# Seven quarter products for the first two blocks of the leading expert, with their gates and the sums around them moved

## The chip, the cores and the metric

The kernel runs on one core of a Trainium2 chip. The metric is device time in microseconds (us) of one execution; a lower time is better. All data are fp32.

## The reference

The first half is a gated linear recurrence over 4 x 8 sequences of 768 steps with a head size of 48. The second half treats the 3072 rows of the result (384 numbers each) as tokens, gives each to the one of 8 experts whose embedding is nearest in angle, and puts it through that expert's two-layer network.

```python
for t in range(S):                       # B, H, S, D = 4, 8, 768, 48
    state = alpha[:, :, t, :, None] * state + einsum('bhd,bhe->bhde', k[:, :, t], v[:, :, t])
    y[:, :, t] = einsum('bhd,bhde->bhe', q[:, :, t], state)
x = y.transpose(0, 2, 1, 3).reshape(B * S, H * D)          # 3072 x 384
logits = (x / (norm(x) + 1e-6)) @ (emb / (norm(emb) + 1e-6)).T / tau
e = argmax(logits, axis=1)
gate = softmax(logits)[arange(N), e]
out = gate[:, None] * (relu(x @ w1[e]) @ w2[e])            # w1: 384 x 1024, w2: 1024 x 384
```

## The kernel before, in words

**Attention part.** The sequence is cut into 24 chunks of 128 steps (`NS`). A software pipeline runs over `s` from 0 to `NS + 2`: in step `s` chunk `s` is turned and its decays are scanned, chunk `s-1` gets its scores and updates the state, chunk `s-2` is mixed (`mix_states`, `mix_chunk`), and chunk `s-3` is turned back into rows (`rows`). At the end of the pipeline, from `s = NS` on, two chunks are in flight at once. Groups of chunks then get their expert (`choose`), their place in the expert's list (`place`), and are sent with an indirect DMA issued by POOL to a sorted copy in memory, `xs` (`to_rows`; the "scatters of rows").

**The leading expert's early blocks.** After chunk 15 it is known that some expert has at least 256 tokens. That expert goes first. Its first two blocks of 128 tokens (`EARLY = 2`) are fetched to `exg` (`fetch_early`) while the attention part still runs, and their first layer (`turn_early`, `first_layer_early`, result `ehT`: 8 slabs of 128 x 256) is spread between the last chunks' work on PE. After the last chunk the counts of the experts are worked out on DVE (`counts`, which ends in `used_i` and `pads`), and blank rows are scattered behind each expert's list (`to_rows(pads...)`).

**Experts.** The second layer of the early blocks runs first: `second_layer` takes 8 products of 384 columns a block. Between the two blocks PE turns the leading expert's last block and half block. Their gates (`gates`: maximum of the logits, squares and root on ACT, exponential on ACT, sum and reciprocal on DVE) are made when the attention part is over. Then `run(i)` goes over the 8 experts: expert 0 has one block left (and a half block in an `If`), the others have three blocks and an `If` for a half block. For three blocks both layers use sums in place of some products. In the second layer, for a pair of blocks, the two blocks are a 2 x 2 grid of quarters of the hidden rows, and `w2` is a 2 x 2 grid of quarters (512 x 192); `second_layer_pair` makes seven products of quarters (Winograd's form) from four sums of hidden quarters (`hT_m`, made by `mix_hidden`) and four sums of weight quarters (`w2_m`, made by `mix_weights`). A product of quarters is four matmuls of 192 columns. Each matmul of fp32 is two instructions in the trace.

**What sets the order.** A planner orders each engine's queue from the program order and its own estimates of readiness. The program pins parts of it: `with tc.issue_after(x)` puts what the block issues behind `x` in `x`'s engine queue, and the lists `pe`, `dve`, `act`, `done_pair` (with `turn_of`, `by_dve`, `by_act`, `pe_turn`) chain calls on one engine. An `If` is one unit in that order.

**Who does which sums before.** `w2_m` for expert 1 is summed by DVE (line 1311); for the experts after it by POOL (line 1313). The sums of the first layer's weights, `w1_m` (`mix_first_weights`), are made by DVE for expert 1 (line 1446), by POOL for the others (line 1357). POOL clears the two tiles `xq` (line 855), into which rows of the experts from 2 on are loaded for turning by DVE.

Of the kernel before, what the change touches and what calls it, by code (L numbers as in the profile page):

```python
# [29 lines left out]
def kernel(  # L30
# [80 lines left out]
    ehT = consts.tile([P, FT, EARLY * P], FP32)  # L111
    NXG = 3
# [113 lines left out]
    with ExitStack() as c1:  # L226
# [79 lines left out]
        def prepare_logits():  # L306

            nc.vector.reciprocal(rtau, rtau)
            e2 = work.tile([E, DM], FP32, name="e2", bufs=1)
            en = work.tile([E, 1], FP32, name="en", bufs=1)  # L310
            nc.scalar.activation(e2, emb, AF.Square, accum_out=en)
# [35 lines left out]
        def choose(g):  # L347

            s0, s1 = GROUPS[g]
            n = s1 - s0  # L350
            shp = [P, n, E]
            l = x_g[g][:, :, LG : LG + E]
            nc.vector.tensor_reduce(
                l.unsqueeze(3), lg_g[g].rearrange("t n j c e -> t n e (j c)"),
                axis=AX.X, op=ALU.add,
            )
            top = work.tile([P, GMAX], FP32, name="top")[:, 0:n]
            nc.vector.tensor_reduce(top.unsqueeze(2), l, axis=AX.X, op=ALU.max)
            win = work.tile([P, GMAX, E], FP32, name="win")[:, 0:n]
            nc.vector.tensor_tensor(win, l, bc(top, shp, 2), ALU.is_equal)  # L360
            nc.vector.tensor_tensor(win, win, bc(first, shp, 1), ALU.mult)
            best = work.tile([P, GMAX], FP32, name="best")[:, 0:n]
            nc.vector.tensor_reduce(best.unsqueeze(2), win, axis=AX.X, op=ALU.max)
            ch = chosen[:, s0:s1]
            nc.vector.tensor_tensor(ch, win, bc(best, shp, 2), ALU.is_equal)
            for s in range(s0, s1):
                eng = nc.vector if {S0 - 1, NS - 1, NS - 2} & set(range(s0, s1)) else nc.gpsimd
                eng.tensor_tensor(before[:, s + 1], before[:, s], chosen[:, s], ALU.add)
# [52 lines left out]
        def counts(n):  # L421
# [20 lines left out]
            nc.vector.scalar_tensor_tensor(  # L442
# [12 lines left out]
            return nc.vector.tensor_copy(used_i, used[0:1])  # L455
# [180 lines left out]
        def mix_chunk(s):  # L636
# [4 lines left out]
            for hh in range(2):  # L641
# [7 lines left out]
                nc.scalar.copy(yT[hh].rearrange("p q t -> p (q t)"), pyx[hh][:, 0:YX])  # L649
# [46 lines left out]
        def first_layer_early(f0, f1):  # L696
            for f in range(f0, f1):
# [6 lines left out]
                nc.scalar.activation(ehT[:, f], ph, AF.Relu)  # L704


# [35 lines left out]
        for s in range(NS + 3):  # L742
# [33 lines left out]
            if NS <= s < NS + 2:  # L776
                with in_turn():
                    first_layer_early(2 * (s - NS), 2 * (s - NS) + 1)
# [16 lines left out]
            if NS <= s < NS + 2:  # L795
                with in_turn():
                    rows(s - 2)
# [31 lines left out]
            if s == NS:  # L829
                with tc.issue_after(st[NS - 1]["masked"].ins):  # L830
                    nc.gpsimd.memset(w1_s[1][:, 0, 0:1], 0.0)
                weights(1)
            for r in rows_of(s):
                g = group_of[r]
                if r == GROUPS[g][1] - 1:
                    with tc.issue_after(st[min(s, NS) - 1]["dve"].ins):
                        choose(g)
                    with behind(s) if s < NS else ExitStack():
                        nc.gpsimd.tensor_copy(x_g[g][:, :, TK], toks[:, slice(*GROUPS[g])])
            if s > NS:  # L840
                with in_turn():
                    first_layer_early(2 * (s - NS) + 2, 2 * (s - NS) + 4)
        with tc.issue_after(st[NS - 1]["dve"].ins):
            routed = [counts(n)]


    with ExitStack() as c3:
        qp = c3.enter_context(tc.tile_pool(name="qp", bufs=1, reuse_waits="tile"))
        xq_s.extend(qp.tile([P, NROW // SQ, DA], FP32, name=f"xq{i}") for i in range(NXQ))
# [10 lines left out]
        yp = c3.enter_context(tc.tile_pool(name="yp", bufs=3, reuse_waits="tile"))  # L860
# [8 lines left out]
        w2_m = wp.tile([P, 4, FT // 2, DM // 2], FP32, name="w2_m")  # L869
        hT_m = xp.tile([P, 4, FT // 2, P], FP32, name="hT_m")  # L870

# [6 lines left out]


# [344 lines left out]
        def second_layer_pair(w2_t, hT, gate, col):  # L1224
# [6 lines left out]
            a, b, d = (bank(j)[:, 0:m] for j in (0, 1, 3))  # L1231
# [28 lines left out]
            gated(y1[:, m:DM], a, g1, u[:, 2])  # L1260
            product(d, s4, b22, False, True)
# [3 lines left out]
            done_pair[:] = pe[0], by_act(nc.scalar.mul, y1[:, 0:m], a, g1)  # L1265
# [34 lines left out]
        def run(i):  # L1300
# [132 lines left out]
        egt = xp.tile([P, EARLY], FP32, name="egt")  # L1433
        esx = xp.tile([P, EARLY], I32, name="esx")
# [49 lines left out]
```

## Time and profile before

| | us |
|---|---|
| median of 3 runs | 392.47 |
| lowest, highest run | 391.89, 395.01 |
| the profiled execution | 391.01 |
| its span, first to last instruction | 389.3 |
| mean granted TensorE clock | 0.998 |

The profiled execution took 391.01 us, of which 1.7 us lie around its span. All times of rows are us from the span's start. PE is the matmul engine; PEld are its weight loads, which overlap the matmuls; DVE, ACT and POOL are the vector, scalar and GpSimd engines; SP issues most DMAs.

### The profile page before, as it was taken

What the parts mean: (1) busy time and instruction counts of PE and PEld (TensorE: products, weight loads), DVE (VectorE), ACT (ScalarE), POOL (GpSimd) and SP (SyncE); (2) the same over time, 40 slices, a digit from 0 to 9 for tenths busy, and PEclk for the clock granted to TensorE, in tenths of its full rate; (3) what the DMA queues carried; (4) which work ended last, traced back from release to release, by engine and by line L of the source; (5) the groups of instructions that cost most, each with busy time, mean ns of one, the idle gap of its engine ahead of it and who ended that gap; (6) DMA issues with size and microseconds to landing.
All of it is one profiled execution on the core that took longest, in us unless ns stands there. A gap on an engine that the chain in (4) does not pass through costs nothing. (4 is left out here: it accounts for less than half of the span.)

```text
span 389.3 us, 12413 instructions
## 1 busy us (share of the span) xinstructions
PE 379.9 (98%) x4596; PEld 338.3 (87%) x4596; DVE 283.9 (73%) x687; ACT 194.3 (50%) x492; POOL 261.7 (67%) x342
## 2 busy tenths in 40 slices
PE   6999999999999999999999999999999999999994
PEld 5889899999999877779989889789979979979974
DVE  7898989889999637992973984963874596795630
ACT  3555565554556544573653734823651492472620
POOL 5365577788776548744829959929957997977201
PEclk9999999999999999999999999999999999999999
DMA  9999999999999996794947768245604810100101
GB/s 138 162 166 166 156 182 197 190 182 198 187 218 174 285 370 231 214 355 97 356 109 285 212 197 287 46 154 182 180 19 175 296 28 18 43 2 17 40 19 46
DMA packets 131181, 64.05 MB, mean 165 GB/s; under 512 B 113319, under 2 KB 127920, under 8 KB 130344
## 3 DMA queue, kind: packets, MB, share of 16 engines
q1 hardware_dynamic: 127008, 52.92, 58.2%
q0 software_dynamic: 3728, 10.16, 7.3%
q8 instruction: 43, 0.70, 0.8%
q14 instruction: 26, 0.21, 0.2%
q10 hardware_dynamic: 376, 0.05, 0.1%
HBM read 53.85 MB, written 11.45 MB: 168 GB/s over the span
## 5 line engine op out<-in xcount | busy, mean ns | idle before, releaser
L1035 DVE TENSOR_TENSOR hT<-hT,pq 128x384 f32<-128x384 f32 x84 | 44.0, 549 | 35.9 <-PE pq L1143 28.4
L889 POOL DMA_INDIRECT out_dram<-y,sx x25 | 29.7, 1188 | 54.3 <-ACTq L1381 20.3
L538 POOL TENSOR_TENSOR qs<-qc,a 128x512 f32<-128x512 f32 x24 | 30.8, 1283 | 30.0 <-DVE a L534 20.8
L1143 PE MATMUL pq<-xT_m,w_m 128*128 128x192 f32 x252 | 44.4, 326 | 0.0
L1017 PE MATMUL pyo<-w,hT 128*128 128x384 f32 x128 | 42.6, 486 | 0.0
L1143 PEld LDWEIGHTS pq<-xT_m,w_m 128*128 128x128 f32 x252 | 41.4, 190 | 0.2
L1017 PEld LDWEIGHTS pyo<-w,hT 128*128 128x128 f32 x128 | 24.1, 190 | 14.8
L1040 ACT ACTIVATE hT<-hT 128x384 f32<-128x384 f32 x56 | 26.3, 515 | 15.2 <-DVE hT L1035 14.6
L1097 POOL TENSOR_TENSOR w_m<-w,w_m 128x256 f32<-128x256 f32 x42 | 31.1, 753 | 2.0 <-PE pq L1143 0.6
L1055 POOL TENSOR_TENSOR w_m<-w 128x768 f32<-128x768 f32 x12 | 23.9, 1991 | 11.7 <-PE pq L1240 11.7
L335 POOL DMA_INDIRECT xs<-x,dest x24 | 24.3, 1013 | 10.4 <-DVE dest L392 5.0
L534 DVE TENSOR_TENSOR_SCAN a<-pa,ini 128x512 f32<-128x512 f32 x24 | 29.3, 1222 | 1.0
L505 DVE TENSOR_TENSOR_SCAN r<-pa,inr 128x511 f32<-128x511 f32 x24 | 29.3, 1220 | 0.7
L1097 POOL TENSOR_TENSOR w_m<-w 128x256 f32<-128x256 f32 x36 | 28.2, 800 | 2.2 <-DVE xT_m L1113 1.4
L1240 PE MATMUL pq<-w_m,hT_m 128*128 128x192 f32 x168 | 28.6, 327 | 0.0
L1240 PEld LDWEIGHTS pq<-w_m,hT_m 128*128 128x128 f32 x168 | 27.4, 190 | 0.5 <-issue 0.5
L217 PE MATMUL pyx<-sm,vt 128*64 128x128 f32 x384 | 26.3, 279 | 0.0
L217 PE MATMUL sc<-qs,kr 64*64 64x128 f32 x768 | 25.6, 271 | 0.0
L217 PEld LDWEIGHTS pyx<-sm,vt 128*64 128x64 f32 x384 | 20.5, 136 | 4.1 <-issue 3.6
L1040 ACT ACTIVATE hT<-pq 128x384 f32<-128x384 f32 x28 | 13.7, 490 | 17.8 <-PE pq L1143 17.8
L1247 DVE SCALAR_TENSOR_TENSOR y<-pq,gt,u 128x192 f32<-128x192 f32 x21 | 8.6, 416 | 18.8 <-PE pq L1240 12.8
L1240 PEld LDWEIGHTS pq<-w,hT 128*128 128x128 f32 x112 | 18.4, 190 | 4.5 <-issue 2.6
(231 smaller groups left out, 986.2 us busy)
## 6 DMA issues: line engine op xcount, KB each, us to landing
w<-in_moe_w_dram SPq DMA_DIRECT2D x12, 1536.0 KB
w<-in_moe_w_dram SPq DMA_DIRECT2D x16, 384.0 KB
at<-in_alpha_dram SPq DMA_DIRECT2D x24, 192.0 KB
kt<-in_k_dram SPq DMA_DIRECT2D x24, 192.0 KB
qt<-in_q_dram SPq DMA_DIRECT2D x24, 192.0 KB
vt<-in_v_dram SPq DMA_DIRECT2D x24, 192.0 KB
xg<-xs SPq DMA_DIRECT2D x22, 196.5 KB
xq<-xs SPq DMA_DIRECT2D x72, 48.0 KB
```

What stands on the lines that cost most here:

```text
L217: last["pe"] = nc.tensor.matmul(*args, **kwargs)
L335: ins = nc.gpsimd.indirect_dma_start(out=xs, out_offset=bass.IndirectOffsetOnAxis(ap=rows, axis=0), in_=x, in_offset=None, bounds_check=E ...
L505: nc.vector.tensor_tensor_scan(r[:, L - 2 :: -1], pa[:, L - 1 : 0 : -1], inr[:, L - 2 :: -1], 1.0, ALU.mult, ALU.add,)
L534: d["a_scan"] = by_dve = nc.vector.tensor_tensor_scan(a, pa, ini, 0.0, ALU.mult, ALU.add)
L538: by_pool = nc.gpsimd.tensor_tensor(qs.rearrange("p n t -> p (n t)"), d["qc"], a, ALU.mult)
L889: ins = nc.gpsimd.indirect_dma_start(out=out, out_offset=bass.IndirectOffsetOnAxis(ap=col, axis=0), in_=y, in_offset=None, bounds_check=N - 1,
L1017: pe[:] = [nc.tensor.matmul(py, lhsT=hT[:, f], rhs=w2_t[:, f], start=(f == 0), stop=(f == FT - 1),)]
L1035: dve[:] = [call(*args, **kwargs)]
L1040: act[:] = [call(*args, **kwargs)]
L1097: by(w[to], w[x], w[y], op)
L1143: pe[:] = [nc.tensor.matmul(to[:, f], lhsT=w[left][:, f * P : (f + 1) * P], rhs=x[right], start=start and f == 0, stop=stop, skip_group_ch ...
L1240: pe[:] = [nc.tensor.matmul(to, lhsT=left[:, f], rhs=right[:, f], start=start and f == 0, stop=stop and f == n - 1, skip_group_check=True,)]
```

## The change

- The early blocks' second layer is made by `second_layer_pair`: seven products of quarters, four sums of `w2_s[0]`'s quarters and four sums of `ehT`'s quarters, all eight on DVE. Two weight sums (`t1`, `t3`) are pinned into the attention part's last steps; the other six stand in a chain on DVE behind `counts`, and the sums of expert 1's first layer stand behind that chain.
- The turning of the leading expert's other rows and their gates (`prepare_lead`) are called in the middle of the pair, behind its fifth product on PE.
- The early blocks' own gates (`early_gates`) are made in step `s = NS`: squares on ACT behind the first early slab and behind the mixing of a late chunk, exponential on ACT behind that chunk's rows, the rest on DVE.
- The sums of expert 1's `w2` go from DVE to POOL, behind the early blocks' scatters and that of expert 0's last block (`done_pair`).
- `xq` is cleared by four copies on ACT in place of two memsets on POOL.
- In memory: `w2_m`, `xq` and `hT_m` are the first tiles after the attention part's tiles are given up; the small tile `e2` is replaced by part of a tile `vt`; the four banks `pq` are laid out first, and the pair uses banks 3, 1 and 2.

```diff
@@ in the attention part @@
+        def early_gates():
+            ...
+            v.tensor_reduce(top_e.unsqueeze(2), l, axis=AX.X, op=ALU.max)
+            v.tensor_scalar(none_e, token, 1.0, float(FAR), ALU.is_lt, ALU.mult)
+            v.scalar_tensor_tensor(
+                out=esx.unsqueeze(2), in0=token, scalar=-1.0, in1=none_e,
+                op0=ALU.add, op1=ALU.add,
+            )
+            v.tensor_tensor(sh_e, l, bc(top_e, shp, 2), ALU.subtract)
+            for t in range(EARLY):
+                nc.scalar.activation(
+                    x2_e, exg[:, t, 0:DM].rearrange("p (h d) -> p h d", d=D), AF.Square,
+                    accum_out=sq_e[:, t],
+                )
+                yield
+            nc.scalar.activation(sq_e, sq_e, AF.Sqrt)
+            v.tensor_scalar(sq_e, sq_e, 1e-6, None, ALU.add)
+            v.reciprocal(sq_e, sq_e)
+            yield v.tensor_tensor(sh_e, sh_e, sq_e.to_broadcast(shp), ALU.mult)
+            nc.scalar.activation(sh_e, sh_e, AF.Exp)
+            yield
+            v.tensor_reduce(egt.unsqueeze(2), sh_e, axis=AX.X, op=ALU.add)
+            v.tensor_scalar(egt, egt, 1e-9, None, ALU.add)
+            yield v.reciprocal(egt, egt)
...
+            if s == NS:
+                gating = early_gates()
+                with tc.issue_after(turned_up.ins), tc.issue_after(st[NS - 1]["dve"].ins):
+                    next(gating)
...
-                    mix_chunk(s - 2)
+                    cols_done = mix_chunk(s - 2)
+                if s == NS:
+                    with tc.issue_after(cols_done.ins):
+                        next(gating)
+                        scaled = next(gating)
...
-                    rows(s - 2)
+                    copied = rows(s - 2)
+                if s == NS:
+                    with tc.issue_after(copied.ins):
+                        next(gating)
...
-                        choose(g)
+                        group_done = choose(g)
+                    if s == NS:
+                        with tc.issue_after(group_done.ins):
+                            early_gated = next(gating)
@@ between the parts @@
-        for x in xq_s:
-            with tc.issue_after(routed[-1].ins):
-                nc.gpsimd.memset(x, 0.0)
...
+        for j in range(4):
+            ps_q.tile([P, 512], FP32, name=f"pq{j}")
@@ second_layer_pair(w2_t, hT, gate, col, middle=None) @@
-            a, b, d = (bank(j)[:, 0:m] for j in (0, 1, 3))
+            a, b, d = (bank(j)[:, 0:m] for j in ((3, 1, 2) if middle else (0, 1, 3)))
...
             product(a, s3, t3, False, False)
             gated(y1[:, m:DM], a, g1, u[:, 2])
+            if middle:
+                middle()
             product(d, s4, b22, False, True)
...
-            done_pair[:] = pe[0], by_act(nc.scalar.mul, y1[:, 0:m], a, g1)
+            if middle:
+                by = nc.vector.tensor_scalar(y1[:, 0:m], a, g1, None, ALU.mult)
+            else:
+                by = by_act(nc.scalar.mul, y1[:, 0:m], a, g1)
+            done_pair[:] = pe[0], by
@@ run(i) @@
-                if i == 1:
-                    mix_weights(w2_t, lambda *args: by_dve(nc.vector.tensor_tensor, *args))
-                else:
+                with turn_of(done_pair if i == 1 else []):
                     mix_weights(w2_t, nc.gpsimd.tensor_tensor)
@@ before the loop over the experts @@
-        known = gates(exg[:, 0:EARLY], egt[:, 0:EARLY], esx[:, 0:EARLY], EARLY)
-        for t in range(EARLY):
-            if t == EARLY - 1:
-                for b in range(len(slots(0))):
-                    prepare(0, b)
-                ready = [prepare_gates(0)]
-            second_layer(
-                w2_s[0], ehT[:, :, t * P : (t + 1) * P], egt[:, t : t + 1], esx[:, t : t + 1]
-            )
-
-        with turn_of([known]):
+        def clear(i, h):
+            x = xq_s[i][:, h * NQR : (h + 1) * NQR]
+            return nc.scalar.copy(x, bc(blank[:, 0:DA], [P, NQR, DA], 1))
+
+        with turn_of([early_up]):
+            clear(0, 0)
+
+        def prepare_lead():
+            with turn_of(act):
+                clear(0, 1)
+            for b, (t, n) in enumerate(slots(0)):
+                turn(
+                    xg_s[0][:, b], xT_s[0][:, :, b * P : b * P + n], n, nc.vector.tensor_copy
+                )
+            ready.append(prepare_gates(0))
...
+        with turn_of([scaled]):
+            nc.vector.tensor_tensor(t1, b12, b11, ALU.subtract)
+        with turn_of([group_done]):
+            nc.vector.tensor_tensor(t3, b22, b12, ALU.subtract)
+        dve[:] = routed[0:2]
+        for to, x, y, op in (
+            (t2, b22, t1, ALU.subtract), (s1, a21, a22, ALU.add), (s2, s1, a11, ALU.subtract),
+            (s3, a11, a21, ALU.subtract), (s4, a12, s2, ALU.subtract),
+            (t4, b21, t2, ALU.subtract),
+        ):
+            by_dve(nc.vector.tensor_tensor, to, x, y, op)
+        mixed = list(dve)
+        second_layer_pair(w2_s[0], ehT, egt, esx, prepare_lead)
+
+        with turn_of(ready):
+            for h in range(2):
+                clear(1, h)
+
+        with turn_of(mixed):
             mix_first_weights(1, nc.vector.tensor_tensor)
```

## Rows read from the trace of the kernel before

**Rows 1.** The page, part 1: busy us, share of the span, instructions.

```profile
PE 379.9 (98%) x4596; PEld 338.3 (87%) x4596; DVE 283.9 (73%) x687; ACT 194.3 (50%) x492; POOL 261.7 (67%) x342
```

**Rows 2.** Stretches: length; busy us of PE, PEld, DVE, ACT, POOL; clock; DMA.

```profile
130.61:150.53 19.92, 19.87 (x263) 16.30 (x260) 8.03 (x43) 7.82 (x27) 11.20 (x15) 1.00 1.03 354
150.53:161.55 11.02, 11.02 (x40) 6.84 (x39) 9.81 (x31) 7.21 (x15) 9.17 (x8) 1.00 0.50 149
161.55:173.43 11.88, 11.88 (x78) 9.76 (x77) 11.52 (x40) 7.00 (x20) 6.86 (x7) 1.00 0.98 335
```

**Rows 3.** Waits of PE's weight loads, whole span: total, times, longest.

```profile
PEld pyx L217 <- issue: 7.6, 41, 0.3
PEld pq L1240 <- issue: 3.1, 9, 0.4
```

**Rows 4.** Timeline of PE: last placing, early second layer, a later pair.

```profile
147.49 0.28 PE L217 MATMUL pyx<-before,ones 128*128 128x8 f32 x2
...
150.75 6.61 PE L1017 MATMUL pyo<-w,ehT 128*128 128x384 f32 x20
157.20 0.96 PE L917 MATMUL pxg<-ident,xg 128*128 128x128 f32 x6
...
166.57 0.50 PE L917 MATMUL pxg<-ident,xg 128*128 128x128 f32 x3
...
200.65 4.06 PE L1240 MATMUL pq<-w_m,hT_m 128*128 128x192 f32 x24
204.54 1.46 PE L1240 MATMUL pq<-w,hT_m 128*128 128x192 f32 x8
```

**Rows 5.** Timeline of DVE: last group, counts, weight sums, hidden sums.

```profile
146.63 0.17 DVE L368 TENSOR_TENSOR before<-before,chosen 128x8 f32<-128x8 f32 x1
...
150.54 0.17 DVE L442 SCALAR_TENSOR_TENSOR pads<-turn_f,pad_row 128x8 int32<-128x8 f32 x1
...
150.81 0.95 DVE L1035 TENSOR_TENSOR w_m<-w 128x768 f32<-128x768 f32 x1
...
154.56 2.35 DVE L910 TENSOR_SCALAR gsq<-gsq 128x2 f32<-128x2 f32 x1 [0.91 <-ACT gsq L910]
...
157.53 0.17 DVE L910 TENSOR_REDUCE gtop<-xg 128x2 f32<-128x16 f32 x1 [0.21 <-DMA xg<-xs]
...
165.85 1.01 DVE L919 COPY xT<-pxg 128x384 f32<-128x384 f32 x2
...
194.44 1.82 DVE L1035 TENSOR_TENSOR hT_m<-hT 128x512 f32<-128x512 f32 x2
...
197.22 0.68 DVE L1035 TENSOR_TENSOR hT_m<-hT_m,hT 128x512 f32<-128x512 f32 x1
```

**Rows 6.** Timeline of ACT: a late chunk's mixing, the last early slab, a table load.

```profile
141.97 0.81 ACT L649 COPY ycols<-pyx 128x256 f32<-128x256 f32 x2 [0.87 <-ACT ehT L704]
...
150.95 0.38 ACT L704 ACTIVATE ehT<-phe 128x256 f32<-128x256 f32 x1 [0.91 <-PE phe L217]
...
154.54 1.28 ACT L910 ACT_TABLE_LOAD   x1
```

**Rows 7.** Timeline of POOL: scatters of rows, memset, a scatter of results, weight sums.

```profile
145.68 0.97 POOL L335 DMA_INDIRECT xs<-x,dest  x1 [0.77 <-DVE x L353]
...
149.51 0.97 POOL L335 DMA_INDIRECT xs<-x,dest  x1 [0.31 <-issue]
150.99 1.61 POOL L335 DMA_INDIRECT xs<-blank,pads  x1 [0.50 <-DVE none L910]
...
154.48 2.40 POOL L855 MEMSET xq<- 128x1344 f32 x2
...
198.96 0.99 POOL L889 DMA_INDIRECT out_dram<-y,sx  x1 [3.85 <-ACTq L1381]
203.50 1.80 POOL L1055 TENSOR_TENSOR w_m<-w 128x768 f32<-128x768 f32 x1 [3.55 <-PE pq L1240]
```

**Rows 8.** Timeline of SP: fetches of the rows of experts 0 and 1.

```profile
154.17 5.77 SPq L184 DMA_DIRECT2D xg<-xs  x6
```

More of the change, by code (lines that the diff above doesn't have):

```diff
@@ L367, in choose @@
                 eng = nc.vector if {S0 - 1, NS - 1, NS - 2} & set(range(s0, s1)) else nc.gpsimd
-                eng.tensor_tensor(before[:, s + 1], before[:, s], chosen[:, s], ALU.add)
+                done = eng.tensor_tensor(before[:, s + 1], before[:, s], chosen[:, s], ALU.add)
+            return done
         def place(g, total=False):
@@ L648, in mix_chunk @@
                     )
-                nc.scalar.copy(yT[hh].rearrange("p q t -> p (q t)"), pyx[hh][:, 0:YX])
+                done = nc.scalar.copy(yT[hh].rearrange("p q t -> p (q t)"), pyx[hh][:, 0:YX])
+            return done
         def rows(s):
@@ L703, in first_layer_early @@
                     )
-                nc.scalar.activation(ehT[:, f], ph, AF.Relu)
+                done = nc.scalar.activation(ehT[:, f], ph, AF.Relu)
+            return done
+        x2_e = at_s[0][:, :, 0:D]
+        sq_e = work.tile([P, EARLY, 1], FP32, name="sq_e", bufs=1)
+        sh_e = work.tile([P, EARLY, E], FP32, name="sh_e", bufs=1)
+        top_e = work.tile([P, EARLY], FP32, name="top_e", bufs=1)
+        none_e = work.tile([P, EARLY, 1], FP32, name="none_e", bufs=1)
+        def early_gates():
+            shp = [P, EARLY, E]
+            l = exg[:, 0:EARLY, LG : LG + E]
+            token = exg[:, 0:EARLY, TK : TK + 1]
+            v = nc.vector
+            v.tensor_reduce(top_e.unsqueeze(2), l, axis=AX.X, op=ALU.max)
[6 more added lines that the diff above has]
+            for t in range(EARLY):
+                nc.scalar.activation(
+                    x2_e, exg[:, t, 0:DM].rearrange("p (h d) -> p h d", d=D), AF.Square,
[11 more added lines that the diff above has]
+            yield v.reciprocal(egt, egt)
         def warm(n):
@@ L830 @@
                 with tc.issue_after(st[NS - 1]["masked"].ins):
-                    nc.gpsimd.memset(w1_s[1][:, 0, 0:1], 0.0)
+                    marked = nc.gpsimd.memset(w1_s[1][:, 0, 0:1], 0.0)
                 weights(1)
@@ L841 @@
                 with in_turn():
-                    first_layer_early(2 * (s - NS) + 2, 2 * (s - NS) + 4)
+                    early_up = first_layer_early(2 * (s - NS) + 2, 2 * (s - NS) + 4)
         with tc.issue_after(st[NS - 1]["dve"].ins):
-            routed = [counts(n)]
+            routed = list(counts(n))
     with ExitStack() as c3:
-        qp = c3.enter_context(tc.tile_pool(name="qp", bufs=1, reuse_waits="tile"))
-        xq_s.extend(qp.tile([P, NROW // SQ, DA], FP32, name=f"xq{i}") for i in range(NXQ))
+        mp = c3.enter_context(tc.tile_pool(name="mp", bufs=1, reuse_waits="tile"))
+        w2_m = mp.tile([P, 4, FT // 2, DM // 2], FP32, name="w2_m")
+        xq_s.extend(mp.tile([P, NROW // SQ, DA], FP32, name=f"xq{i}") for i in range(NXQ))
+        hT_m = mp.tile([P, 4, FT // 2, P], FP32, name="hT_m")
+        yp = c3.enter_context(tc.tile_pool(name="yp", bufs=3, reuse_waits="tile"))
         for i in range(2):
@@ L1222, in first_layer_blocks, with second_layer_pair @@
             squares()
-        def second_layer_pair(w2_t, hT, gate, col):
+        def second_layer_pair(w2_t, hT, gate, col, middle=None):
             n, m = FT // 2, DM // 2
@@ L1430, in run_rest @@
                         half_block(w1_t, w2_t, xT, gate[0:HALF], col[0:HALF])
-        egt = xp.tile([P, EARLY], FP32, name="egt")
-        esx = xp.tile([P, EARLY], I32, name="esx")
-        known = gates(exg[:, 0:EARLY], egt[:, 0:EARLY], esx[:, 0:EARLY], EARLY)
-        for t in range(EARLY):
-            if t == EARLY - 1:
-                for b in range(len(slots(0))):
-                    prepare(0, b)
-                ready = [prepare_gates(0)]
-            second_layer(
-                w2_s[0], ehT[:, :, t * P : (t + 1) * P], egt[:, t : t + 1], esx[:, t : t + 1]
-            )
-        with turn_of([known]):
+        ready = []
+        NQR = NROW // SQ // 2
+        def clear(i, h):
[9 more added lines that the diff above has]
+                    xg_s[0][:, b], xT_s[0][:, :, b * P : b * P + n], n, nc.vector.tensor_copy
+                )
+            ready.append(prepare_gates(0))
+        (b11, b12), (b21, b22) = quarters(w2_s[0])
+        (a11, a12), (a21, a22) = (hidden(ehT, t) for t in range(2))
+        t1, t2, t3, t4 = (w2_m[:, k] for k in range(4))
+        s1, s2, s3, s4 = (hT_m[:, k] for k in range(4))
+        with turn_of([scaled]):
[15 more added lines that the diff above has]
+        with turn_of(mixed):
             mix_first_weights(1, nc.vector.tensor_tensor)
```

15 lines of the change are left out of this document (7 added, 8 removed).

## The prediction

> **What bounds the kernel now.** I read the page's shares first: PE is busy 98% of the span, DVE 73%, POOL 67%, ACT 50% [rows 1]. A busy PE can hide waits, so the second view is the list of what PE's weight loads waited for. Over the whole span its two largest rows are waits for "issue", none longer than 0.4 us; the first belongs to the attention part, and the second are the nine breaks in the experts' pairs [rows 3]. From the early blocks on nothing in that list is a wait for DVE, ACT, POOL or a DMA. Third, the stretches: from 150.53 to 161.55, where the code changes most, PE has work for all 11.02 us, and the clock is granted in full (1.00, the level of 2.4 GHz) there, before and behind [rows 2]. So the time is what PE has to do, one thing after the other, and work taken from another engine is worth nothing by itself. The change can gain only what it takes from PE, and it can lose wherever a sum, a gate or a fetch now comes later than PE.
>
> DVE needs a look of its own. It is busy 9.81 of 11.02 us and then 11.52 of 11.88 us around the early blocks, but only 8.03 of 19.92 us in the attention part's last steps [rows 2]. Work moved from the first two stretches into the third lies in idle time; work added to the first two may make DVE the late engine.
>
> **PE: products of 384 columns become products of 192.** Before, two blocks take 8 matmuls each, 32 instructions of 384 columns. Twenty of them and the turning start 6.45 us apart (157.20 less 150.75), so one takes 0.3225 us and 32 take 10.32 us [rows 4]. After, seven products of four matmuls are 56 instructions of 192 columns. In a later pair 24 such start 3.89 us apart from the next kind (204.54 less 200.65), 0.162 us each [rows 4]; 56 take 9.08 us. Half a matmul costs half the time in these rows to within 1%, so the eighth that is left out is nearly all kept. PE gains 10.32 - 9.08 = 1.24 us. The six matmuls of turning are the same before and after.
>
> **DVE: eight sums on the path of the pair.** The first two products take unmixed quarters, 16 instructions, 2.59 us; the third wants `s2` and `t2`. If PE starts at 150.75 as before, that is at 153.34. The chain for it starts behind `pads`, which ends at 150.71 [rows 5]; then come `t2` (a weight sum, 0.95 us), `s1` and `s2` (0.68 us each when alone), which ends at 153.02 [rows 5]. `s1` also wants the last slab of `ehT`, ready at 151.33 [rows 6], before DVE gets there. The other end is from the two hidden sums that took 1.82 us together in a later pair, 0.91 us each [rows 5]: `s2` at 153.48, and with 0.2 us for the handing over (an estimate, from the 0.28 us between the end of `pads` and the POOL instruction that uses it [rows 5, 7]) 153.7. So PE waits between 0 and 0.4 us. I take 0.1: nothing on POOL runs long there but the scatter of blank rows, beside which the 0.95 was measured. The later sums (`s3`, `s4`, `t4`) follow every 0.7 to 0.95 us while PE takes a product every 1.30 us, so they gain on it.
>
> **The turning in the middle of the pair.** It stands behind the fifth product, 40 instructions behind 150.75: 157.23, where it began before at 157.20 [rows 4]. It wants the rows that SP fetches from 154.17 on [rows 8]; DVE's wait for both blocks' rows ended at 157.53 [rows 5], and the second block is turned some 0.35 us behind the first. The cost is 0 to 0.3 us; I take 0.05. The products behind are pinned behind the turning, so a late fetch stops PE.
>
> **DVE behind the pair.** Off DVE go the early gates with the instruction that took 2.35 us beside POOL's memset [rows 5, 7], two of the four weight sums, and two scalings; on it come four hidden sums (2.7 us) and four smaller scalings (0.4 us each is an estimate, from 0.51 us for each copy of 384 columns from the same kind of bank [rows 5]). The balance is some 3 us less. But the 16 sums of expert 1's first layer now stand behind the chain. The copies of expert 1's turned rows (165.85) follow those sums on DVE, and the third turning, at 166.57, uses the bank that the first of them empties [rows 4, 5]: a margin of some 0.2 us before. PE will now be there about 1.2 us earlier. If DVE is too, nothing is lost; if it stands still at 165.85, PE waits up to 1 us. With DVE freed of some 3 us I take 0.1 and keep 0.5 as the upper end.
>
> **Gates into the attention part.** ACT gets two squares, a root and an exponential with its table load of 1.28 us [rows 6] between chunks; before a late mixing copy it sat idle 0.87 us [rows 6], so a load of 1.28 us makes the next copy late by some 0.4 us at most, while PE has a block of other work in between. DVE gets some ten small instructions and two weight sums (1.9 us) in a stretch where it is 40% busy. Cost 0, if they lie in the gaps; the cover is DVE's wait for PE, and what it costs if it fails is the second rival.
>
> **POOL.** The two memsets go (2.40 us), and nobody on PE waited for them. ACT's four copies that replace them are needed only when rows for expert 2 are fetched. The sums of expert 1's `w2` come to POOL: four of 1.80 us, 7.2 us, behind the early scatters and the one of expert 0. POOL sat idle 3.85 us before the scatter at 198.96 and 3.55 us before the next sums at 203.50 [rows 7], 7.4 us in all, so the first layer's sums for expert 2, which ended at 195.1 (198.96 less 3.85), end near 195.1 + 7.2 = 202.3; PE wants them from about 207.1 (204.54 and 16 instructions of 0.162). `t2` of expert 1 is wanted at 200.65 and comes first. Cost 0 with some 4 us of room.
>
> **Memory.** The pair's banks are 3, 1 and 2. Its second product writes bank 1, at 150.75 and 8 x 0.162, 152.05; that bank's last slab of `ehT` is read out by 151.33 [rows 6]. The tiles that `w2_m` and `hT_m` now lie on belong to the last chunks at the latest, whose products PE has ended before 147.49 [rows 4], and `e2` is used in the first steps alone. Cost 0; a wait here would stand in the pair, and 0.4 us, the upper end of the sums' wait, covers it.
>
> **The sum.** -1.24 + 0.10 + 0.05 + 0.10 = -0.99 us. Against the profiled execution's own 391.01 us that is 390.0. The median of the three runs stands 1.46 us above that execution, so as a median I give 391.5.
>
> **Rivals.** *First, the gain is eaten by waits behind the pair's start* (late sums 0.4, late rows 0.3, late copies 0.5: 1.2 us). For it speaks how full DVE is [rows 2] and the narrow margins at 153.3 and 166.6; against it, that three upper ends meet. It gives 391.0 in the profile, a median of 392.4.
>
> *Second, slower: the pinned weight sums delay the scatters and so the fetch that the pair waits for.* The scatter of blank rows took 1.61 us beside DVE's weight sums, others 0.97 us [rows 5, 7], so a sum beside a scatter costs POOL 0.64 us. Two sums beside the scatters from 140 on cost 1.28 us, less the 0.77 us for which POOL waited before 145.68: 0.5 us. And if `t3` falls in front of the last group's work on DVE, 0.95 us go into the chain from there to `pads`; PE's next placing has 0.69 us of room (146.80 to 147.49 [rows 4, 5]), the fetch has nearly none. Together 1.5 us at the fetch, less 0 to 0.3 us of room: net of -1.24 and the 0.15 us of other waits, 0.1 to 0.5 us slower, a median near 392.9; it decides once the rows land more than 1.3 us later than 157.53.
>
> On this the Trainium skill (SBUF — State Buffer, section "Who interferes with whom") says that a DVE instruction with two inputs in SBUF contends with a GpSimd instruction that reads SBUF, and that the one which comes later is held up until the first is done. The stretched scatter agrees with it. By that rule, with each of the six scatters from 145.68 to the blank ones meeting a sum, the loss would be larger than in the rival; but only two sums are put there.
>
> *Third, POOL becomes the bound for expert 1 or 2*, because the `If` of expert 0 or a scatter is queued badly with the new sums: some 2 us slower (7.2 less the room of 4, and 1 for a scatter), a median of 394. The room speaks against it.
>
> **How the numbers follow.** Forecast (0.6 to 1.3 us faster) 0.62; first rival 0.20; second 0.13; third 0.03; a gain above 1.3 us 0.02, since PE has no wait there to give back. One per cent, about what a measurement of this kernel can tell from no change, is 3.9 us. None of the cases reaches it by itself; I leave 0.02 for faster and 0.04 for slower, the larger because a bad order on a queue has no upper end in these rows. The range goes from the profiled execution with the full gain, 391.01 - 1.24 = 389.8, to the second rival's 392.9 with 0.5 us for the scatter of medians (the three runs lie 3.1 us apart): 389.8 to 393.4.
>
> **What the changed profile would show.** The 56 instructions of the pair in place of the 32, and the leading expert's first layer starting 1.0 to 1.2 us earlier in the span than before; weight loads before the third product with a wait of at most 0.1 us named after DVE `hT_m`; turning at 157.2 to 157.5; `pads` still ending near 150.7 and SP's first fetch at 154.2; two weight sums on DVE between 137 and 145; POOL's sums of 768 columns done before 191. The prediction is wrong if PE reaches 150.75 later than before, if a wait above 0.4 us stands in or behind the pair, or if the shift of 1 us is lost before the end, which would mean that PE isn't what binds later.

## The result, and the profile after

The changed kernel takes 398.83 us, the median of 6 runs (396.63 to 399.96); the kernel before takes 393.61 us in the 6 runs beside them. The ratio is 1.0135, with an interval of 1.0091 to 1.018. The change makes the kernel slower by some 5 us; the forecast was 391.5 us. Ratios, here and below, leave out slow runs, those over 1.5% above the fastest of the same kernel, so they can differ a little from the quotient of two medians. The profiled execution is one of 399.96 us, with a span of 398.3 us.

The page's first part answers to [rows 1]:

```profile
PE 381.7 (96%) x4620; PEld 344.3 (86%) x4620; DVE 293.2 (74%) x693; ACT 197.9 (50%) x499; POOL 268.5 (67%) x344
```

PE's share falls from 98% to 96%: PE now stands still somewhere. The view of what its weight loads waited for says how long, as [rows 3] did for before (total, times, longest):

```profile
PEld pq L1295 <- issue: 9.9, 11, 6.7
PEld pyx L219 <- issue: 7.1, 39, 0.3
```

The pairs' row had 3.1 us in nine waits of at most 0.4 before; now one of them alone is 6.7 us. PE's timeline shows where, first over the early blocks, then over expert 1's pair (answering to [rows 4]):

```profile
150.03 2.76 PE L1295 MATMUL pq<-w,ehT 128*128 128x192 f32 x16
152.63 4.06 PE L1295 MATMUL pq<-w_m,hT_m 128*128 128x192 f32 x24
156.53 0.91 PE L972 MATMUL pxg<-ident,xg 128*128 128x128 f32 x6
157.28 1.47 PE L1295 MATMUL pq<-w,hT_m 128*128 128x192 f32 x8
158.58 1.46 PE L1295 MATMUL pq<-w_m,ehT 128*128 128x192 f32 x8
159.88 1.39 PE L1058 MATMUL pq<-xT,w 128*128 128x128 f32 x11
...
202.56 1.46 PE L1295 MATMUL pq<-w,hT_m 128*128 128x192 f32 x8
210.41 2.90 PE L1295 MATMUL pq<-w_m,hT 128*128 128x192 f32 x8 [6.39 <-DVE y L1302]
213.10 2.31 PE L1198 MATMUL pq<-xT,w 128*128 128x192 f32 x8
215.25 1.46 PE L1198 MATMUL pq<-xT,w_m 128*128 128x192 f32 x8
```

The early pair runs without a break and 1.27 us faster than the blocks it replaces (9.85 us from 150.03 to 159.88; before, 11.12 us from 150.75 to 161.87). It also starts 0.72 us earlier. That lead isn't won there, nor by moving the early gates: it is there, to the hundredth, at the eighth turning of `alpha` in the attention part, first in the changed kernel, then in the one before:

```profile
40.04 0.60 PE L222 MATMUL pa<-ident,at 128*128 128x128 f32 x4
40.76 0.60 PE L220 MATMUL pa<-ident,at 128*128 128x128 f32 x4
```

It arises in the first 25 us. The fifth such turning starts between 23.82 and 24.81 us in all ten traces of kernels with the early pair, and between 25.54 and 26.12 us in the four without it. Which part of the change brings this was not tested. At 202.56 PE is still 1.98 us ahead of before, where the same products began at 204.54 [rows 4]. Then the last product of expert 1's pair waits for one of DVE's gated sums into `y`. DVE's timeline of that moment:

```profile
202.28 0.35 DVE L1168 TENSOR_TENSOR xT_m<-xT,xT_m 128x192 f32<-128x192 f32 x1
202.55 4.36 DVE L1173 TENSOR_TENSOR xT_m<-xT 128x192 f32<-128x192 f32 x2
206.84 1.97 DVE L1160 SCALAR_TENSOR_TENSOR xT_m<-xT_m 128x192 f32<-128x192 f32 x1
208.73 0.88 DVE L1178 TENSOR_TENSOR xT_m<-xT 128x192 f32<-128x192 f32 x3
209.53 1.06 DVE L1302 SCALAR_TENSOR_TENSOR y<-pq,gt,u 128x192 f32<-128x192 f32 x3
```

and POOL's:

```profile
199.55 1.52 POOL L1152 TENSOR_TENSOR w_m<-w 128x256 f32<-128x256 f32 x2
201.85 1.12 POOL L944 DMA_INDIRECT out_dram<-y,sx  x1 [0.78 <-issue]
202.98 1.84 POOL L1110 TENSOR_TENSOR w_m<-w 128x768 f32<-128x768 f32 x1
204.90 1.80 POOL L1110 TENSOR_TENSOR w_m<-w,w_m 128x768 f32<-128x768 f32 x1
206.66 1.93 POOL L1110 TENSOR_TENSOR w_m<-w 128x768 f32<-128x768 f32 x1
```

The two are to be read together. DVE's 13 row sums (`xT_m`, sums of the turned rows for expert 2's first layer) take 0.35 us each where nothing holds them up. But the three that stand beside POOL's three weight sums take 6.3 us together (2.49, 1.95 and 1.97 us), each ending 0.2 us behind one of POOL's. The three gated sums into `y` that empty the pair's banks, the memory to which PE writes its products, stand behind the row sums on DVE's queue; the first starts at 209.53, and PE goes on at 210.41. The stretches show what the standstill does to the clock (length; busy us of PE, PEld, DVE, ACT, POOL; clock; DMA):

```profile
199.50:210.00 10.50, 4.52 (x28) 4.22 (x26) 10.32 (x16) 0.84 (x2) 8.17 (x6) 0.90 0.59 197
210.00:216.50 6.50, 6.09 (x24) 6.12 (x25) 0.92 (x3) 1.38 (x3) 3.84 (x4) 0.63 1.04 381
216.50:226.00 9.50, 9.50 (x61) 9.50 (x60) 7.31 (x16) 4.90 (x12) 8.50 (x12) 1.00 0.40 92
```

Behind the standstill the granted clock is at its lower level (1.2 of 2.4 GHz) for a while: the mean is 0.63 in the second stretch, and the first eight instructions there start 0.34 us apart, twice the usual 0.162. The 24 instructions from 210.41 to 216.55 take 6.14 us; at 0.162 us each they would take 3.9. So the stretch costs 6.66 us of wait and 2.2 us of slow clock. Less the 1.98 us gained before it, PE is 6.9 us behind, and it stays so to its last weight load (390.79 against 383.86 us). Another 2 us stand behind that load (7.5 us to the end against 5.5). This tail is 5.3 to 5.6 us in some of the traces below and 6.7 to 7.5 us in others, those of the kernel before among both, so I don't put it down to the change.

### The profile page after: what moved, and what is told of

Read it like the earlier page. It is cut to its first block, busy times and chain, and to the rows that moved or that the text cites. A ratio compares the mean times of both kernels' runs of the same rounds, so it can differ in the third digit from the quotient of the medians.

```text
span 398.3 us, 12478 instructions
## 1 busy us (share of the span) xinstructions
PE 381.7 (96%) x4620; PEld 344.3 (86%) x4620; DVE 293.2 (74%) x693; ACT 197.9 (50%) x499; POOL 268.5 (67%) x344
## 5 line engine op out<-in xcount | busy, mean ns | idle before, releaser
L1152 POOL TENSOR_TENSOR w_m<-w,w_m 128x256 f32<-128x256 f32 x42 | 32.0, 774 | 2.2 <-PE pq L1198 0.8
L1110 POOL TENSOR_TENSOR w_m<-w 128x768 f32<-128x768 f32 x14 | 27.0, 1937 | 8.9 <-PE pq L1295 8.8
L1295 PE MATMUL pq<-w_m,hT_m 128*128 128x192 f32 x192 | 32.7, 327 | 0.0
L339 POOL DMA_INDIRECT xs<-x,dest x24 | 25.2, 1049 | 9.9 <-DVE dest L397 5.0
L1295 PEld LDWEIGHTS pq<-w_m,hT_m 128*128 128x128 f32 x192 | 31.3, 190 | 0.6 <-issue 0.6
L1152 POOL TENSOR_TENSOR w_m<-w 128x256 f32<-128x256 f32 x36 | 27.4, 776 | 3.1 <-DMA w<-in_moe_w_dram 2.0
L1110 POOL TENSOR_TENSOR w_m<-w,w_m 128x768 f32<-128x768 f32 x14 | 25.5, 1823 | 2.2 <-PE pq L1295 1.6
L219 PE MATMUL sc<-qs,kr 64*64 64x128 f32 x768 | 26.5, 277 | 0.0
```

The lines of the kernel that those rows point to most:

```text
L219: last["pe"] = nc.tensor.matmul(*args, **kwargs)
L1110: by(to, x, y, ALU.subtract)
L1152: by(w[to], w[x], w[y], op)
L1295: pe[:] = [nc.tensor.matmul(to, lhsT=left[:, f], rhs=right[:, f], start=start and f == 0, stop=stop and f == n - 1, skip_group_check=True,)]
```

## The experiments

The theories named in the expectations. **A**: POOL's sums of expert 1's `w2`, queued behind the `If` of expert 0, push POOL's later sums beside DVE's hidden and row sums; sums of both engines that read two operands from the on-chip memory hold each other up, and the gated sums behind them come late. **B**: the rest of the change does it. **C**: POOL is simply late for PE. All runs after the first comparison were on three other chips; the kernel before takes 400 to 404 us there, and each ratio is against its runs on the same chip.

**One part undone.** Expert 1's four sums go back to DVE, as before; the pair stays:

```diff
-                with turn_of(done_pair if i == 1 else []):
+                if i == 1:
+                    mix_weights(w2_t, lambda *args: by_dve(nc.vector.tensor_tensor, *args))
+                else:
                     mix_weights(w2_t, nc.gpsimd.tensor_tensor)
```

> The changed kernel, with the four sums of expert 1's w2 back on DVE (chained there, as in the kernel before); all else as changed. Theory A (POOL's added sums keep POOL running beside DVE's sums for expert 2, both stretch, the three scalings of expert 1's pair stand behind them on DVE and PE waits 6.4 us, then runs 2.1 us longer at a lower clock): the wait is gone, ratio to before 0.994 to 0.998, PE's first product of expert 2 about 2 us earlier than before. Rival B (the early pair, its gates or the moved tiles cost the time): stays near 1.013.

Measured: 401.39 us against 400.45, ratio 0.9994 (0.9948 to 1.0039), just above the 0.994 to 0.998 expected by A and far from B's 1.013. The wait in expert 1's pair is gone. But a wait that the first trace doesn't have stands in the early pair:

```profile
PEld pq L1295 <- ACT u L1095: 6.9, 1, 6.9
PEld pq L1295 <- issue: 3.1, 9, 0.4
```

**That part done alone.** The kernel before, with nothing changed but that expert 1's sums are on POOL:

```diff
-                if i == 1:
-                    mix_weights(w2_t, lambda *args: by_dve(nc.vector.tensor_tensor, *args))
-                else:
+                with turn_of(done_pair if i == 1 else []):
                     mix_weights(w2_t, nc.gpsimd.tensor_tensor)
```

> The kernel before, with one part of the change alone: the four sums of expert 1's w2 on POOL behind the scatter of expert 0's last block. POOL's order around expert 1 is then that of the changed kernel. Theory A: PE waits 4 to 8 us in the last product of expert 1's pair, ratio to before 1.015 to 1.025 (the loss of the change without the 1.2 us that the early pair gives). Rival B: 1.000, within 0.3%.

Measured: 406.78 us, ratio 1.0127 (1.0045 to 1.0209), a little under the 1.015 to 1.025 expected. Without any early pair, PE's loads show the same wait, at the same product:

```profile
218.24 2.42 PEld L1240 LDWEIGHTS pq<-w_m,hT 128*128 128x128 f32 x8 [6.64 <-issue]
```

and DVE's row sums the same shape ahead of it (4.35 us for two, 1.95 for the next). B falls for the wait in expert 1's pair: this one edit makes it.

**The sums earlier, and the next sums later.** In the first kernel POOL makes expert 1's sums right behind the early pair, ahead of expert 0's scatters; in the second, expert 2's sums are queued behind a scatter of expert 1's pair:

```diff
+        with turn_of(done_pair):
+            mix_weights(w2_s[1], nc.gpsimd.tensor_tensor)
...
-                with turn_of(done_pair if i == 1 else []):
+                with turn_of(done_pair if i == 1 else first_sent if i == 2 else []):
```

> The changed kernel, with the four sums of expert 1's w2 still on POOL but called right behind the early pair, so that they stand on POOL's queue ahead of the scatter of expert 0's last block and of the If. Theory A (what costs is when POOL does them, not that POOL does them): no wait of PE in expert 1's pair, ratio to before 0.994 to 0.999. Rival B: near 1.013. Rival C (POOL has too much work for expert 1 and 2 wherever the sums stand): a wait of several us remains, ratio above 1.005.

> The changed kernel, with POOL's sums of expert 2's w2 pinned behind the first scatter of expert 1's pair, so that three long POOL sums no longer run beside DVE's last sums for expert 2. POOL gets later by it. Theory A (the stretch comes from both engines running two-input sums at once): DVE's 13 small sums take about 4 us in place of 9.5, PE waits 0 to 2 us, ratio to before 0.995 to 1.003. Rival C (POOL's lateness itself is what PE waits for): PE waits as long or longer, ratio 1.013 or above.

Measured: 406.96 us, ratio 1.0136 (1.0049 to 1.0223), for the first; the second's four runs lie between 400.87 and 413.31 us and give no verdict, so its trace is used only for where waits stand. In both the wait left its place and came up in another, so the first missed what A expected of it (no loss) and, by its time alone, fits C. Its trace shows a hold-up of the same kind in another place. With the sums early, PE waits 5.1 us for turned rows that DVE copies (179.7 us). Before that copy DVE stood in one small scaling of the gates while POOL made three of the weight sums:

```profile
172.52 5.90 DVE L965 TENSOR_SCALAR gt<-gt 128x2 f32<-128x2 f32 x1
173.04 3.58 POOL L1110 TENSOR_TENSOR w_m<-w 128x768 f32<-128x768 f32 x2
176.57 1.81 POOL L1110 TENSOR_TENSOR w_m<-w,w_m 128x768 f32<-128x768 f32 x1
```

So A's wording is too narrow: this instruction reads one operand, and it was held through three sums, not one. With the next sums later, expert 1's pair waits 1.3 us, and expert 2's pair waits 5.2 us, again behind two row sums that take 3.85 us and one of 1.95.

**The changed kernel again, POOL held back, and POOL busy without reading.** Three kernels on one chip: the changed kernel as it is; one in which POOL, before the `w2` sums of each expert from 2 on, copies one column of the last row sum, so that it must wait for DVE; and one in which fills (`memset`, which writes and reads nothing) stand in place of expert 2's sums.

> The changed kernel itself, once more, on the chip of the two that run beside it. Theory A (GpSimd's lately queued weight sums hold VectorE's row sums up in expert 1's pair): the one wait of TensorE of 6 to 7 us in expert 1's pair stands again, and the time is 1 to 2% above the kernel before. A rival on the first series of experiments (the early pair itself brings a wait of its own, of 3.5 to 7 us, released by ScalarE's gated copy): that wait shows here too, and on a chip where it shows the time is 2 to 3% above. If the early pair has no such wait here, the waits of that series belong to its chip and not to the change.

```diff
+                if i > 1:
+                    seen = yp.tile([P, 1], FP32, name="seen", bufs=1)
+                    nc.gpsimd.tensor_copy(seen, sum_x(16)[:, 0:1])
                 with turn_of(done_pair if i == 1 else []):
```

> The changed kernel, with one more instruction on GpSimd ahead of the four w2 sums of each expert from 2 on: a copy of one column of the last row sum, so that GpSimd starts them only behind VectorE's 13 row sums (a copy of four columns took 0.2 us in the trace of before). GpSimd is later by this, not earlier. Theory A: the row sums of expert 2 run at some 0.35 us each but for those beside the w1 sums (0.6 to 0.9), the last ends near 204 us instead of 209.6, TensorE's wait of 6.66 us in expert 1's pair falls under 1.5 us, the clock stays up, and the time is 6 to 8 us under the changed kernel, within 0.5% of before. Rival C (GpSimd's lateness by itself makes the wait, wherever its sums stand): the wait stays at 6 us or grows.

```diff
-                    mix_weights(w2_t, nc.gpsimd.tensor_tensor)
+                    if i == 2:
+                        for k in range(4):
+                            for _ in range(3 - k % 2):
+                                nc.gpsimd.memset(w2_m[:, k], 0.0)
+                    else:
+                        mix_weights(w2_t, nc.gpsimd.tensor_tensor)
```

> The changed kernel, with the four w2 sums of expert 2 left out: ten fills of the same quarters stand on GpSimd in their place (some 0.75 us each by the 1.24 us of a fill of 1344 columns, 7.5 us in all, as long as the sums), which read nothing from the memory. Expert 2's second blocks are therefore computed from zeros. Theory A: GpSimd is busy as long and as late as in the changed kernel, but VectorE's row sums beside the fills take 0.35 us, and the wait of 6.66 us in expert 1's pair falls under 1.5 us; the time is 6 to 8 us under the changed kernel. Rival C (lateness or a busy GpSimd by itself): row sums beside fills are as slow as beside sums, the wait stays at 5 us or more.

Measured: the changed kernel 412.02 us, ratio 1.0273 (1.0207 to 1.0339), with the wait of 6.65 us in expert 1's pair and waits of 3.6 and 2.5 us in the early pair; POOL held back 404.98 us, 1.0105 (1.0016 to 1.0195); fills 404.56 us, 1.0076 (1.0033 to 1.0119). Both take 7.0 to 7.5 us off, and in both PE's wait in expert 1's pair is 1.29 us. With POOL held back the time isn't within the 0.5% of the kernel before that was expected: the early pair's own waits, 9.1 us in that trace, remain. With fills, DVE's row sums beside a busy POOL:

```profile
215.39 0.61 DVE L1173 TENSOR_TENSOR xT_m<-xT 128x192 f32<-128x192 f32 x2
215.93 0.35 DVE L1160 SCALAR_TENSOR_TENSOR xT_m<-xT_m 128x192 f32<-128x192 f32 x1
216.20 0.88 DVE L1178 TENSOR_TENSOR xT_m<-xT 128x192 f32<-128x192 f32 x3
```

```profile
215.79 5.08 POOL L1375 MEMSET w_m<- 128x768 f32 x7
```

POOL is as busy and as late as in the changed kernel (its first fill starts 0.40 us behind the first of these six row sums; its first sum started 0.43 us behind it there), and the sums take 0.35 us. In the other kernel POOL is later still (219.10 us), and that costs nothing. C falls, A holds: it is what POOL reads beside DVE's sums. The remaining 1.29 us stand behind sums that still run beside POOL's sums for the first layer: the last two hidden sums, 1.26 and 1.10 us against 0.68 and 0.69 before, and the first two row sums, 1.66 us together.

**Half of the sums.** Two of expert 1's sums on POOL, two on DVE:

```diff
-                with turn_of(done_pair if i == 1 else []):
+                if i == 1:
...
+                        if len(made) > 2:
+                            return by_dve(nc.vector.tensor_tensor, *args)
+                        with turn_of(done_pair):
+                            return nc.gpsimd.tensor_tensor(*args)
```

> The changed kernel with two of expert 1's four w2 sums on GpSimd (3.6 us in place of 7.2) and two on VectorE. GpSimd's w1 sums of expert 2 should end some 3.6 us earlier than in the changed kernel (at 197.5 on its scale), before VectorE's row sums begin. Theory A, in which the price is set by how many row sums are still to come when GpSimd's first w2 sum of expert 2 starts: at most two are held up, the wait in expert 1's pair is 0 to 3 us, under half of 6.66. If the price went with GpSimd's added work instead, it would be half, 3.3 us.

Measured: 412.01 us, ratio 1.0226 (1.0183 to 1.0269). The wait in the pair is gone altogether, neither half of 6.66 us nor a part of it. But the fourth sum, on DVE, needs the second, on POOL, and DVE stood still for it while the whole first layer of expert 1 was queued behind, which cost PE 6.2 us:

```profile
198.91 2.14 DVE L1090 TENSOR_TENSOR w_m<-w,w_m 128x768 f32<-128x768 f32 x1 [5.45 <-POOL w_m L1379]
```

That standstill came before the row sums and let POOL catch up 6.2 us on PE, more than the 3.6 us by which its work was cut, so neither the time nor the missing wait of this run settles how the price goes with the amount of work.

**The early pair's own wait.** In all eight traces of kernels with the early pair on the three other chips, PE waits in that pair in front of products that follow ACT's copies `u` (3.5 to 9.1 us in all; some of the waits are put down to `u`, some to no releaser), and in the first trace it doesn't. To see whose wait it is, the pair alone was run again beside a traced run of the kernel before on the same chip:

> The changed kernel with the four w2 sums of expert 1 left on VectorE, where the kernel before has them: the early pair alone, once more, beside a traced run of the kernel before on the same chip. Theory A: no wait in expert 1's pair, and its share of the change is the early stage: 0.7 to 1.3 us under the kernel before where the early pair runs without a wait of its own (as in the first trace of the changed kernel), ratio 0.997 to 0.999. A rival (the early pair's own wait belongs to the pair): the wait of 3.5 to 7 us released by ScalarE's gated copy stands in the early pair in this trace as well, the kernel before has none there on this chip, and the ratio is 1.00 to 1.01.

> The kernel before, unchanged, for its trace on this chip. If results of TensorE reach ScalarE late around the early blocks here too (ScalarE's copies over 1 us behind the end of the products that they read), the lateness is the chip's, and what the pair adds is that TensorE waits for it; if not, the pair brings it.

Measured: the pair alone 404.31 us, ratio 1.0044 (1.0012 to 1.0076); its early pair waits twice:

```profile
152.98 2.68 PEld L1295 LDWEIGHTS pq<-w,ehT 128*128 128x128 f32 x16
157.23 2.57 PEld L1295 LDWEIGHTS pq<-w_m,hT_m 128*128 128x128 f32 x16 [1.57 <-ACT u L1095]
167.38 2.42 PEld L1295 LDWEIGHTS pq<-w_m,hT_m 128*128 128x128 f32 x8 [7.57 <-ACT u L1095]
```

ACT's two copies started at 166.91 us, though the products that they read had been started by 159.8. DVE is late too: its first gated sum, at 163.32 us, reads the second product, started by 156.0, and the copy that ended at 157.18:

```profile
156.76 0.42 ACT L1095 ACTIVATE u<-pq,egt 128x192 f32<-128x192 f32 x1 [2.02 <-PE pq L1295]
166.91 0.73 ACT L1095 ACTIVATE u<-pq,egt 128x192 f32<-128x192 f32 x2 [9.73 <-remote]
163.32 0.42 DVE L1302 SCALAR_TENSOR_TENSOR y<-pq,egt,u 128x192 f32<-128x192 f32 x1 [5.43 <-remote]
```

The kernel before (403.12 us, one run) has no break in its early blocks there:

```profile
158.78 6.21 PEld L1017 LDWEIGHTS pyo<-w,ehT 128*128 128x128 f32 x20
```

So the wait comes with the pair, as the rival said: its third and fifth products accumulate in a bank that ACT must have read first, while before no product of the early blocks' second layer waits for ACT. But the lateness is not the pair's alone. In the same trace of the kernel before, ACT's first copy of the first layer that follows comes 3.65 us behind the start of the product (162.79 against 161.87, 0.92 us, in the trace of the first chip), and PE waits for it there:

```profile
170.47 1.50 PE L1003 MATMUL pq<-xT,w 128*128 128x128 f32 x12
174.12 0.28 ACT L1007 ACTIVATE hT<-pq 128x128 f32<-128x128 f32 x1 [3.37 <-PE pxg L917]
174.45 0.74 PEld L1003 LDWEIGHTS pq<-xT,w 128*128 128x128 f32 x6 [0.66 <-ACT hT L1007]
```

What the pair adds is that PE has to wait for a late result earlier and longer. In the pair alone POOL issues its scatters of blank rows all through this time, the last of them at 164.15 us, just before the late copy. That gave a last pair of kernels: six of the eight scatters moved behind the early output scatters, with the pair alone and with the kernel before (theory **D**: results come late as long as these scatters run; **E**: something else in the pair delays them):

```diff
+        early_sent = list(done_pair)
...
-                to_rows(pads[:, i + 2 : i + 3], blank)
+                with turn_of(early_sent):
+                    to_rows(pads[:, i + 2 : i + 3], blank)
```

> The early pair alone (expert 1's w2 sums on VectorE), with six of the eight pads scatters put behind the early pair's two output scatters on GpSimd's queue, so that only two run beside the pair; nothing is left out. Theory D (on the chips where the early pair waits, results of TensorE reach ScalarE late as long as GpSimd's pads scatters run): the waits of 5 to 9 us in the early pair shrink to under 2 us and the time is 4 to 8 us under that of the pair alone, ratio to the kernel before 0.98 to 0.995. Rival E (the lateness comes from something else in the pair, such as its copies or its DVE sums): the waits stay at 5 us or more and the ratio stays at 1.00 to 1.01.

> The kernel before, with the same six pads scatters put behind its early output scatter: the control to the run beside it. Its early blocks show no wait of TensorE, so both theories expect its time within 0.5% of the kernel before; if it is over 0.5% faster, the move pays by itself and not through the pair.

Measured: the pair alone with late scatters 398.23 us, ratio 0.9894 (0.9825 to 0.9962); the kernel before with late scatters 399.96 us, 0.9941 (0.9902 to 0.998). In the first the waits of 9.1 us have shrunk to one of 2.7, where D had expected under 2:

```profile
158.95 5.55 PEld L1295 LDWEIGHTS pq<-w_m,hT_m 128*128 128x128 f32 x24 [2.70 <-ACT u L1095]
```

It ends 1.5 us behind the last of the two scatters that were left beside it:

```profile
156.44 1.05 POOL L339 DMA_INDIRECT xs<-blank,pads  x1 [0.30 <-issue]
167.56 1.09 POOL L944 DMA_INDIRECT out_dram<-y,esx  x1 [10.07 <-DVE gsq L965]
```

E falls on that chip, and D holds in the main: moving the scatters takes most of the lateness away. But results don't stay late as long as scatters run: with the sums early, PE got its result at 159.54 us and made the next three products without a wait, while POOL issued such scatters until 166.28. The move pays 0.6% without the pair too, where D and E had expected under 0.5%. Together it is the best version here, by its ratio some 4 us faster than the kernel before; of this the pair's share over the moved scatters alone is 0.5% by the two ratios, whose intervals overlap, so it isn't shown.

## Why the prediction was wrong

**PE** was right: 1.24 us were forecast, 1.27 came. PE also started the early pair 0.72 us earlier, which the prediction had no term for; the lead is made in the first 25 us of the kernel and is luck as far as the forecast goes.

**DVE's eight sums, the turning in the middle, the copies behind the pair, the gates and the memory** were right on the first chip. `s2` ended at 152.32 us, before PE's weight loads took it at 152.47; the turning follows without a wait, and no wait above 0.41 us stands from the pair up to 202 us. Only the gates, put at 0, cost PE a wait of 0.33 us, at 137.34 us, behind their root on ACT. On the other chips the pair waits for ACT; the prediction had no term for a product's own result coming late, and the trace of before, from the first chip, didn't show one.

**POOL** is the step that failed: "The sums of expert 1's `w2` come to POOL: four of 1.80 us" and "Cost 0 with some 4 us of room". Its time was right: the first layer's sums for expert 2 were put near 202.3 us and ended at 201.07, before PE wanted them. What it left out is who works beside POOL. The room of 4 us was counted to PE's need. Before, these sums ended at 195.1, just as DVE began its hidden sums, and POOL's next weight sums ran while DVE had 0.83 us of work in 5.50:

```profile
203.50:209.00 5.50, 5.50 (x36) 5.50 (x35) 0.83 (x2) 1.62 (x4) 5.38 (x3) 1.00 0.51 161
```

The added 7.2 us pushed them beside DVE's hidden and row sums. The first two row sums, at 199.63 us, took 1.66 us beside POOL's sums for the first layer, and at 202.55 six of the 13 were still to come, 1.6 us of work, when POOL's first `w2` sum for expert 2 started at 202.98. Before, all 13 were done at 203.03, and that sum started at 203.50 [rows 7]. So a lateness of 1.2 us (204.2 against 203.0) cost 5.4 us: three row sums took 6.3 us in place of 0.8, since each ended only behind a sum of 1.8 to 1.9 us. Nor did the prediction follow a late row sum on to PE: the gated sums that free the pair's banks stand behind the row sums on DVE, and no term was made for that.

The hint was in the prediction itself. It had two hidden sums taking 0.91 us in a later pair where one alone takes 0.68 [rows 5], and used them as the upper end of another term. It also quoted the Trainium skill (SBUF — State Buffer, section "Who interferes with whom"): a DVE instruction with two inputs in that memory contends with a GpSimd instruction that reads it, and the later one is held up until the first is done. It applied this to the scatters alone. The runs agree on the price: 0.35 us for a row sum beside fills or nothing, 1.95 to 2.49 us beside a sum. On the order they don't: by the trace the first row sum held up starts at 202.55 us, before POOL's sum at 202.98. Of GpSimd instructions that only write, the same section says that such a DVE instruction doesn't contend with them; the fills above agree.

The three rivals were wrong as well. The third, POOL as the bound for expert 1 or 2, named the engine, but its price was for POOL coming late to PE, and in the run where POOL is held back even longer the time falls by 7 us. Its sum doesn't come out either: 7.2 less 4 and 1 more is 4.2 us, some 3 net of the gain and not 2, and the room of 4 us had been counted behind the 7.2 already.

**Size.** On the chip with the three kernels, taking the collision away gives 7.0 us (404.98 against 412.02). Taken from 398.83 us this would leave 391.8 us on the first chip (an estimate from runs on two chips), near the 391.5 forecast. The nearness is in part luck: the figure holds a gain that the sum didn't have, the lead of 0.72 us, and against it a loss that it didn't have either, the 1.29 us of wait left in expert 1's pair.

## What to carry to other kernels

A sum moved to an idle engine has to be priced beside what the other engine of the pair will be doing when it really runs: list DVE's two-input instructions and POOL's reading instructions on one time scale, with the shift that the move brings, and count how many of the short ones meet a long one. Each such meeting cost about the length of the long one here (1.6 to 2.1 us beside sums of 1.8 to 1.9), and once a small scaling stood 5.90 us beside three of them, so a lateness of 1.2 us can cost 5. Then follow the queue behind the held instruction to the one that frees a bank for PE, and count a standstill of PE twice, once for itself and once for the slower clock behind it (here 6.7 and 2.2 us).

## What the runs showed of the hardware that was not expected

Results of TensorE reach ScalarE and VectorE late in the early pair on three of the four chips, where POOL scatters rows by index: products started by 159.8 us were read at 166.91. The moving of six scatters takes most of it away on the one chip where that was tried. On the first chip, eight such scatters were issued from 150.47 to 163.1 us, six of them beside the same pair, without any wait. Why the chips differ, and whether it is the scatter's issue or its transfers, is not settled by these runs.
